# An attention and feed-forward kernel on one core: the planner's last slot of a round takes a VectorE step by its announced length

## The chip, the cores and the metric

One core of a Trainium2 chip runs the whole program. Times are device microseconds (us) of one execution. The kernel before took 1028.57 us, the median of 3 runs (1028.46 to 1028.59). The execution that the profiler recorded took 1029.18 us; its span, from the first to the last recorded instruction, is 1027.4 us, and the 1.78 us around it belong to no instruction of the program. A difference of under 0.2% (2.06 us) is called no change here.

## The reference

Two stages. The first is attention with a sigmoid in place of the softmax, for 8 batches, 12 heads, 448 positions and heads of 64 elements; the second is a feed-forward network over the 3584 rows that come out of it.

```
scores = scale * np.matmul(q, k.transpose(0, 1, 3, 2)) - np.log(S)
attn = 1.0 / (1.0 + np.exp(-scores))
attn_out = np.matmul(attn, v)                      # 8 x 12 x 448 x 64
x = attn_out.transpose(0, 2, 1, 3).reshape(B*S, H*D)   # 3584 x 768
h = x @ w_in                                       # 768 -> 2048
g = np.maximum(0.01 * h, h)
out = g @ w_out                                    # 2048 -> 768
```

All of it is float32. The kernel gets the weights as 64-bit words and decodes them itself.

## The kernel before

**Precision.** TensorE multiplies a rounded form of float32. Each operand is therefore split into a high part (a cast) and a low part (the operand less its high part), and a product is three matmuls: high by high, high by low, low by high. ScalarE makes most high parts, VectorE nearly all low parts (`low`, lines 202, 502, 607).

**Attention.** 48 pairs of heads are worked off in 24 rounds of two pairs (lines 794 to 814). Counted from 0, round r works on pairs 2r and 2r+1, called x and y, in five slots: scores of x, scores of y, x by its values, y by its values, and a last slot (`ending`) with the 64 positions that are left over of both. Scores go to PSUM in four buffers of two banks that are used in turn (tag `s`, line 767); a round takes nine of them: three for the scores of x, three for y, one each for the two products with the values, and one for the left-over scores. So the second score tile of a round takes the buffer in which the round before kept the product `pv` of its pair x. That buffer is free when VectorE has added it to the result in `keep` (lines 577 to 579), and the two `keep` additions of a round are put at the head of the next round's first slot (line 575). In slots 2 to 4 VectorE and ScalarE split the queries and keys of the next round's two pairs: the high part of the first in slot 2, its low part and the high part of the second in slot 3, the low part of the second in slot 4 (lines 805 to 807).

**The decoding.** Beside this VectorE decodes the weights, in the generator `prep` (lines 388 to 444). It is cut into steps, one VectorE instruction each, with a `yield` behind each. A weight block has four pieces; a piece takes three short instructions and two long ones on 128x384 words (lines 423 to 432). Behind the fourth piece of a `w_in` block come four long sums (`firsts`, lines 343 to 352), behind that of a `w_out` block a list of sums of 192, 384 or 576 words (`second`, lines 358 to 386). Some yields are free: they stand for no instruction, such as the nine behind each `w_in` block (`rest`). DMAs that load raw pieces and store results are issued by SyncE from inside the steps, and SyncE's queue keeps the program's order.

**The planner.** The program is written out in one order for each engine; nothing is reordered afterwards. Every VectorE instruction adds its length to a count called `queue`, by a formula: 0.14 us and its words at 960 or 1920 a us (lines 145 to 155). At the end of a slot `prepare(pace, time)` (lines 449 to 455) adds the pace to a credit, puts in steps while there is a credit of 1 and the count is more than 0.2 below the slot's time (`LESS`), and takes the slot's time off the count, down to zero at most. The slots' times are 1.92, 1.92, 2.33, 2.33 and 1.66. A step put in just under the limit may end well above it, and what is above the slot's time is carried into the next slot. After the attention, `fill` (lines 457 to 462) puts up to four steps into each of the products of the first matmul stage, by the same count against 1.8 us.

**After the attention.** The first matmul of the network is done in 4 quarters of 56 products of 9 matmuls with seven-product (Strassen) sums, the second in 52 products of 36 matmuls. Each weight tile of the first is cast and its low part taken about two products ahead.

Of the kernel before, what the change touches and what calls it, by code (L numbers as in the profile page):

```python
# [30 lines left out]
PACES = 4, 5, 4.2, 2.8, 2  # L31
TIMES = 1.92, 1.92, 2.33, 2.33, 1.66
PRODUCT, LESS, MOST = 1.8, 0.2, 4
WAIT, REST = 9, 3
FFN = 126
ALONE = 100
# [29 lines left out]
PLAIN = {0: (), 1: (("store", "d", 0, 4, 0),), 2: (("store", "d", 4, 2, 4),)}  # L66
STEPS = (
# [34 lines left out]
def attn_ffn_kernel(ctx: ExitStack, tc: tile.TileContext, qk, v, w_in, w_out, out):  # L102
# [40 lines left out]
    queue = 0.0  # L143
# [13 lines left out]
    def sub(to, x, y):  # L157
        vec(out=to, in0=x, in1=y, op=ALU.subtract)
# [10 lines left out]
    def later(slots, *fns, first=False):  # L169

        chores.setdefault(now + slots, ([], []))[not first].extend(fns)
# [162 lines left out]
    def block(dtype, shape, name, pool=None):  # L334

        pool, tag, size, bufs = pool or (pp, "w", 4 * HW, 2)
        a, b = shape
        t = pool.tile([P, size], F32, tag=tag, name=name, bufs=bufs)[:, :a * b]
        return (t if dtype == F32 else t.bitcast(dtype)).rearrange("p (a b) -> p a b", a=a, b=b)
# [3 lines left out]
    def firsts(u, dec):  # L343
        to = td[u // 2][:, :, u % 2]
        dma(out=to[:, :3], in_=dec[:, 1:])

        b12, b22, b11, b21 = (dec[:, i] for i in range(4))
        sums = block(F32, (4, HW), f"ws0_{u}")
        for place, x, y in ((2, b12, b11), (0, b22, sums[:, 2]), (1, b22, b12), (3, b21, sums[:, 0])):
            sub(sums[:, place], x, y)  # L350
            yield
        dma(out=to[:, 3:], in_=sums)

    def rest():

        return (None for _ in range(WAIT if now < FFN else REST))

    def second(u, k, dec):


        n = len(BLOCKS)
        size = wide // 2
        e, at = u // 2, u % 2 * size
        both = {side: dec[i].rearrange("p a b -> p (a b)").rearrange("p (n m) -> p n m", n=n) for i, side in enumerate("ds")}

        def of(n, side, at, step):
            x = both[side]
            if step == 0:
                return x[:, at:at + 1].broadcast_to((P, n, size))
            end = at + (n - 1) * step + (1 if step > 0 else -1)  # L370
            return x[:, at:end if end >= 0 else None:step]

        for what, *x in PLAIN.get(k, STEPS):
            if what == "wait":
                yield from rest()
            elif what == "store":
                side, i, n, form = x
                dma(out=t2d[:, form:form + n, e, at:at + size], in_=both[side][:, i:i + n])
            else:
                n, fn, *x = x  # L380
                to, x, y = (of(n, *z) for z in x)
                if fn == "neg":
                    vec_st(out=to, in0=x, scalar=-1.0, in1=y, op0=ALU.mult, op1=ALU.subtract)
                else:
                    (add if fn == "add" else sub)(to, x, y)
                yield

    def prep():

        n = 4
        pieces = [(m, k) for m in range(len(todo)) for k in range(n)]
        raws = []

        def load():
            at = len(raws)
            if at == len(pieces):
                return
            m, k = pieces[at]  # L400
            w, u = todo[m]
            size = 4 * HW // n
            pool = (stage, "stage", 2 * HW, STAGE) if at % 2 and now < ALONE else (pp, "wr", 2 * HW, 3)
            raw = block(I32, (size, 2), f"wr{w}_{u}_{k}", pool)
            dma(out=raw.rearrange("p m t -> p (m t)"), in_=(w_in, w_out)[w][u][:, k * size:(k + 1) * size].bitcast(I32))
            raws.append(raw)

        for _ in range(3):
            load()
        yield  # L410
        for at, (m, k) in enumerate(pieces):
            w, u = todo[m]
            if k == 0 and w == 0:
                dec = block(F32, (4, HW), f"wd{w}_{u}")
            elif k == 0:
                both = [block(F32, (4, HW), f"wd{w}_{i}") for i in range(2)] if u == 0 else both[::-1]
                dec = both[0]
            raw = raws[at]
            size = 4 * HW // n
            low, high = raw[:, :, 0], raw[:, :, 1]  # L420
            tf = dec.rearrange("p b m -> p (b m)")[:, k * size:(k + 1) * size]
            t = tf.bitcast(I32)
            vec_s(out=t, in0=high, scalar1=0x7FFFFFFF, scalar2=None, op0=ALU.bitwise_and)
            yield
            vec_s(out=tf, in0=tf, scalar1=W_LEAST, scalar2=W_MOST, op0=ALU.max, op1=ALU.min)
            yield
            vec_s(out=t, in0=t, scalar1=5, scalar2=2, op0=ALU.logical_shift_left, op1=ALU.logical_shift_right)
            yield
            vec_st(out=t, in0=high, scalar=-0x40000000, in1=t, op0=ALU.bitwise_and, op1=ALU.bitwise_or)
            yield  # L430
            vec_st(out=t, in0=low, scalar=29, in1=t, op0=ALU.logical_shift_right, op1=ALU.bitwise_or)
            yield
            while len(raws) < min(at + 1 + (5 if now < ALONE else 3), len(pieces)):
                load()
            if now < ALONE:
                yield
            if w == 1:
                yield from second(u, k, both)
            elif k == n - 1:
                yield from firsts(u, dec)  # L440
            if k == n - 1:
                prepared.add((w, u))
                if w == 0:
                    yield from rest()

    preps = prep()
    credit = 0.0

    def prepare(pace, time):
        nonlocal credit, queue  # L450
        credit += pace
        while credit >= 1 and queue < time - LESS:
            next(preps, None)
            credit -= 1
        queue = max(0.0, queue - time)

# [312 lines left out]
    def go(todo, work):  # L769


        for x, what in todo:
            for y in what.split():
                later(0, lambda x=x, y=y: x.do(y))
        slot(work)

    def whole(x):
        x.scores(0)
        x.scores(1)

    def ending(x, y):

        if y is not None:
            y.last_scores()
        x.last_v()
# [8 lines left out]
    for r in range(rounds):  # L794
        x, y, *more = pairs[2 * r:2 * r + 6]
        works = [lambda: whole(x), lambda: whole(y), x.attn_v, y.attn_v, lambda: ending(y, more[0] if more else None)]
        if r == 0:

            works = [works[2], works[1], x.last_scores, *works[3:]]
        if more:  # L800
            z, w = more[:2]
            how = vcopy if PLAN_ATTN.get((r, 3), "").startswith("h") else copy
            later(0, z.load_v)
            later(1, w.load_v)
            later(2, z.high)
            later(3, z.low, lambda: w.high(how))
            later(4, w.low)
        for n, far in enumerate(more[2:]):
            later(1 + 3 * n, far.load_qk)
        for n, work in enumerate(works):  # L810
            go([(ops[0], PLAN_ATTN.get((r, n), ""))], work)
            for t in EARLY.get((r - rounds + 1, n), ()):
                advance(t)
            prepare(PACES[n] * (r > 0), TIMES[n])

    kept, chores[now] = chores[now][0], ([], chores[now][1])
    for fn in kept:
# [20 lines left out]
    queue = 0.0  # L838
# [146 lines left out]
    ahead = 0  # L985
# [14 lines left out]
    ahead = READY + 2  # L1000

    for k in range(NOP, size):
        m, at = divmod(k - NOP, 12)
# [163 lines left out]
```

## Time and profile before

| what | us |
|---|---|
| median of 3 runs | 1028.57 |
| the profiled execution | 1029.18 |
| its span | 1027.4 |
| TensorE matmuls, busy | 1023.2 (100%) |
| TensorE weight loads, busy | 867.8 (84%) |
| VectorE, busy | 857.2 (83%) |
| ScalarE, busy | 598.1 (58%) |
| granted TensorE clock, mean | 1.000 |

TensorE's matmuls are pipelined and their ends are modelled, so that a gap of some tenths of a microsecond doesn't show in their busy time. The starts of the weight loads, one for each matmul, show it, and the profile says for each idle stretch of the weight loader what ended it; "issue" means that nothing it can see did. The attention fills the span up to 246 us, the first matmul of the network goes from there to 649 us, the second to 1024 us.

### The profile page before, as it was taken

How to read it: one execution, taken by the hardware profiler on the slowest of the kernel's cores; microseconds unless marked ns; L12 is line 12 of the kernel's file. 1: busy time of each engine (PE TensorE's matmuls, PEld its weight loads, DVE VectorE, ACT ScalarE, POOL GpSimd, SP SyncE). 2: the span in 40 equal slices, each digit the busy share in tenths (PEclk: the TensorE clock that was granted, in tenths of full speed). 3: DMA queues.
4: the chain of work that ended last, by engine and by line, in shares of the span. 5: the costliest groups of instructions: out<-in, count | busy, mean ns of one | idle time of the engine just before them, and what ended most of it. 6: DMA issues, size and time to landing. Idle time of an engine off the chain costs nothing.

```text
span 1027.4 us, 16361 instructions
## 1 busy us (share of the span) xinstructions
PE 1023.2 (100%) x6316; PEld 867.8 (84%) x6316; DVE 857.2 (83%) x1015; ACT 598.1 (58%) x634; POOL 0.3 (0%) x5
## 2 busy tenths in 40 slices
PE   9999999999999999999999999999999999999998
PEld 6555555556999999999999999999999999999998
DVE  5889999789998899898975657699988888899883
ACT  7888888887545655555555555565362535444440
POOL 0000000000000000000000000000000000000000
PEclk9999999999999999999999999999999999999999
DMA  8888787989889898989986878997678797767833
GB/s 308 279 298 278 280 281 267 311 292 331 289 312 322 293 298 299 344 317 409 338 296 213 300 283 313 392 408 289 217 282 286 278 416 291 284 221 252 311 113 135
DMA packets 113853, 301.10 MB, mean 293 GB/s; under 512 B 9712, under 2 KB 51696, under 8 KB 113776
## 3 DMA queue, kind: packets, MB, share of 16 engines
q1 hardware_dynamic: 111760, 295.52, 80.5%
q10 hardware_dynamic: 2016, 4.54, 1.2%
q8 instruction: 50, 0.82, 0.3%
q14 instruction: 27, 0.22, 0.1%
HBM read 203.16 MB, written 96.86 MB: 292 GB/s over the span
## 4 chain that ended last, share of the span: by engine, by line
PE 99%; ACT 0%; ACTq 0%; DVE 0%; DVEq 0%; issue 0%
PE px_h L139 22%; PE acc_A L139 18%; PE acc_B L139 18%; PE pv L139 13%; PE pz_h L139 11%; PE sc L139 11%; PE py_h L139 6%; PE acc_one L139 0%; ACTq L139 0%; ACT L139 0%; DVE o L139 0%; ACT qks L139 0%; DVEq L1163 0%; ACT warm L139 0%
## 5 line engine op out<-in xcount | busy, mean ns | idle before, releaser
L139 PE MATMUL px_h<-hi,w 128*128 128x448 f32 x768 | 223.1, 361 | 0.0
L139 PEld LDWEIGHTS px_h<-hi,w 128*128 128x128 f32 x768 | 143.9, 187 | 11.3 <-ACT x L139 0.7
L139 PE MATMUL acc_A<-gh,w 128*128 128x448 f32 x528 | 151.4, 361 | 0.0
L139 DVE TENSOR_TENSOR w<-wx,w 128x768 fp32r<-128x768 f32 x112 | 106.9, 955 | 48.2 <-ACT w L139 48.2
L139 PE MATMUL px_h<-lo,w 128*128 128x448 f32 x384 | 139.4, 363 | 0.0
L139 ACT ACTIVATE s<-sc 128x896 f32<-128x896 f32 x144 | 119.4, 934 | 17.7 <-PE sc L139 17.7
L139 PE MATMUL acc_B<-gh,w 128*128 128x448 f32 x416 | 119.4, 361 | 0.0
L139 PE MATMUL pv<-s,v 64*64 64x448 f32 x1152 | 114.0, 540 | 0.0
L139 PE MATMUL pz_h<-hi,w 128*128 128x448 f32 x384 | 112.7, 361 | 0.0
L139 PEld LDWEIGHTS acc_A<-gh,w 128*128 128x128 f32 x528 | 98.9, 187 | 7.4
L139 PEld LDWEIGHTS sc<-qks 64*128 64x128 f32 x876 | 79.9, 187 | 23.6 <-issue 16.2
L139 ACT CAST w<-wx 128x768 fp32r<-128x768 f32 x112 | 92.0, 834 | 10.8 <-DMA wx<-t 10.8
L139 PE MATMUL sc<-qks 64*128 64x448 f32 (+1 forms) x876 | 95.5, 368 | 0.1
L139 PEld LDWEIGHTS pv<-s,v 64*64 64x64 f32 x1152 | 41.6, 133 | 60.9 <-issue 47.7
L139 DVE TENSOR_TENSOR w<-w 128x1536 fp32r<-128x1536 f32 x52 | 91.1, 1752 | 0.0
L139 ACT ACTIVATE c_h<-c_h 128x896 f32<-128x896 f32 x48 | 45.9, 956 | 74.1 <-DVE c_h L139 74.1
L139 PE MATMUL acc_B<-g,w 128*128 128x448 f32 x328 | 84.8, 362 | 0.0
L139 PEld LDWEIGHTS acc_B<-gh,w 128*128 128x128 f32 x416 | 77.9, 187 | 5.8
L139 ACT CAST w<-w 128x1536 fp32r<-128x1536 f32 x52 | 77.1, 1482 | 0.5 <-DMA w<-t 0.5
L139 PEld LDWEIGHTS pz_h<-hi,w 128*128 128x128 f32 x384 | 71.9, 187 | 5.3
L139 PEld LDWEIGHTS px_h<-lo,w 128*128 128x128 f32 x384 | 72.1, 188 | 3.8
L139 DVE SCALAR_TENSOR_TENSOR wd<-wr,wd 128x384 int32<-128x384 int32 x128 | 71.3, 557 | 3.2
(96 smaller groups left out, 1619.1 us busy)
## 6 DMA issues: line engine op xcount, KB each, us to landing
wx<-t SPq DMA_DIRECT2D x112, 384.0 KB, 5.4
w<-t SPq DMA_DIRECT2D x52, 768.0 KB, 4.3
g<-g SPq DMA_DIRECT2D x34, 896.0 KB, 7.4
g<-c_h SPq DMA_DIRECT2D x60, 448.0 KB, 4.4
g<-s SPq DMA_DIRECT2D x48, 448.0 KB, 5.9
qk<-in_qk SPq DMA_DIRECT2D x46, 456.0 KB, 5.2
g1s<-g SPq DMA_DIRECT2D x18, 896.0 KB, 6.1
wr<-in_w_in SPq DMA_DIRECT2D x32, 384.0 KB, 5.2
```

What stands on the lines that cost most here:

```text
L139: return lambda *args, **kw: tc.keep_in_program_order(issue(*args, **kw))
```

## The change

Each step of the decoding announces how long the next one is: `LONG` (0.54) where the next is a long one, and nothing, which is read as `SHORT` (0.34), elsewhere. The announcement is kept in `ahead`. `prepare` gets a third argument, true in the last of a round's five slots. There a step is put in only if, beside the old condition, the count and the announced length together stay under the slot's time and 0.1 (`OVER`): under 1.76. Credit that is not spent stays. The other four slots and `fill` work as before, and the instructions are the same 1015 on VectorE, in another order.

```diff
+SHORT, LONG, OVER = 0.34, 0.54, 0.1
...
             sub(sums[:, place], x, y)
-            yield
+            yield LONG
...
-        for what, *x in PLAIN.get(k, STEPS):
+        steps = PLAIN.get(k, STEPS)
+        for m, (what, *x) in enumerate(steps):
...
-                yield
+                yield next((z[1] > 1 and LONG for z in steps[m + 1:] if z[0] == "sum"), None)
...
             vec_s(out=t, in0=t, scalar1=5, scalar2=2, op0=ALU.logical_shift_left, op1=ALU.logical_shift_right)
-            yield
+            yield LONG
             vec_st(out=t, in0=high, scalar=-0x40000000, in1=t, op0=ALU.bitwise_and, op1=ALU.bitwise_or)
-            yield
+            yield LONG
             vec_st(out=t, in0=low, scalar=29, in1=t, op0=ALU.logical_shift_right, op1=ALU.bitwise_or)
-            yield
+            yield k == n - 1 and LONG
...
             if now < ALONE:
-                yield
+                yield k == n - 1 and LONG
...
-    credit = 0.0
+    credit, ahead = 0.0, SHORT
 
-    def prepare(pace, time):
-        nonlocal credit, queue
+    def prepare(pace, time, whole):
+        nonlocal credit, queue, ahead
         credit += pace
-        while credit >= 1 and queue < time - LESS:
-            next(preps, None)
+        while credit >= 1 and queue < time - LESS and (not whole or queue + ahead < time + OVER):
+            ahead = next(preps, None) or SHORT
             credit -= 1
         queue = max(0.0, queue - time)
...
-            prepare(PACES[n] * (r > 0), TIMES[n])
+            prepare(PACES[n] * (r > 0), TIMES[n], n == len(works) - 1)
```

## Rows read from the trace of the kernel before

**Rows 1.** The page's first part: busy us (share) and instructions of each engine.

```profile
PE 1023.2 (100%) x6316; PEld 867.8 (84%) x6316; DVE 857.2 (83%) x1015; ACT 598.1 (58%) x634; POOL 0.3 (0%) x5
```

**Rows 2.** Busy time by stretch: window, PE, PEld, DVE, ACT, POOL (instructions), clock, DMA share, GB/s.

```profile
100.00:150.00 50.00, 50.00 (x502) 27.87 (x500) 46.60 (x83) 42.30 (x55) 0.00 (x0) 1.00 0.80 281
400.00:500.00 100.00, 100.00 (x502) 93.73 (x501) 91.47 (x129) 55.69 (x63) 0.00 (x0) 1.00 0.94 349
```

**Rows 3.** Waits of the weight loader, 0 to 260 us: total us, times, longest.

```profile
PEld sc L139 <- DVE x L139: 1.0, 4, 0.4
```

**Rows 4.** Weight loads in order of time: start, us, names, count, idle before and releaser.

```profile
106.40 3.51 PEld L139 LDWEIGHTS sc<-qks 64*128 64x128 f32 x36 [0.70 <-issue]
110.22 0.21 PEld L139 LDWEIGHTS pv<-s,v 64*64 64x64 f32 x8 [0.30 <-ACT s L139]
...
116.39 1.11 PEld L139 LDWEIGHTS sc<-qks 64*128 64x128 f32 x12 [0.70 <-issue]
117.74 2.32 PEld L139 LDWEIGHTS sc<-qks 64*128 64x128 f32 x24 [0.24 <-DVE x L139]
...
126.54 3.51 PEld L139 LDWEIGHTS sc<-qks 64*128 64x128 f32 x36 [0.70 <-issue]
...
136.52 1.11 PEld L139 LDWEIGHTS sc<-qks 64*128 64x128 f32 x12 [0.70 <-issue]
...
146.67 3.51 PEld L139 LDWEIGHTS sc<-qks 64*128 64x128 f32 x36 [0.71 <-issue]
...
176.63 1.11 PEld L139 LDWEIGHTS sc<-qks 64*128 64x128 f32 x12 [0.70 <-issue]
...
186.91 3.51 PEld L139 LDWEIGHTS sc<-qks 64*128 64x128 f32 x36 [0.71 <-issue]
...
236.86 1.11 PEld L139 LDWEIGHTS sc<-qks 64*128 64x128 f32 x12 [0.71 <-issue]
...
240.73 0.21 PEld L139 LDWEIGHTS pv<-s,v 64*64 64x64 f32 x8 [0.30 <-ACT s L139]
```

**Rows 5.** VectorE in order of time, round 9's end and the additions behind it.

```profile
105.59 1.03 DVE L139 TENSOR_TENSOR qks<-qk,qks 128x848 fp32r<-128x848 f32 x1
106.54 0.35 DVE L139 TENSOR_SCALAR wd<-wr 128x384 int32<-128x384 int32 x1
106.81 1.15 DVE L139 TENSOR_TENSOR x<-x,pv 128x448 f32<-128x448 f32 x2
```

**Rows 6.** VectorE, round 10's end and the additions behind it.

```profile
114.59 0.55 DVE L139 TENSOR_TENSOR ws<-wd 128x384 f32<-128x384 f32 x1
115.18 0.56 DVE L139 TENSOR_TENSOR ws<-wd,ws 128x384 f32<-128x384 f32 x1
115.65 1.03 DVE L139 TENSOR_TENSOR qks<-qk,qks 128x848 fp32r<-128x848 f32 x1
116.61 0.55 DVE L139 TENSOR_TENSOR ws<-wd 128x384 f32<-128x384 f32 x1
117.07 1.15 DVE L139 TENSOR_TENSOR x<-x,pv 128x448 f32<-128x448 f32 x2
```

**Rows 7.** VectorE early in the network's first matmul.

```profile
253.74 1.09 DVE L139 TENSOR_TENSOR c_h<-c_h,py_h 128x896 f32<-128x896 f32 x1 [0.82 <-PE py_h L139]
...
256.21 0.95 DVE L139 TENSOR_TENSOR w<-wx,w 128x768 fp32r<-128x768 f32 x1
```

**Rows 8.** The weight loads of product 6, from the first with the low part of its weights.

```profile
257.27 0.39 PEld L139 LDWEIGHTS pz_h<-hi,w 128*128 128x128 f32 x2
```

**Rows 9.** SyncE's queue in order of time, round 10.

```profile
114.70 0.38 SPq L139 DMA_DIRECT2D t<-wd  x1
115.17 0.44 SPq L139 DMA_DIRECT2D qk<-in_qk  x1
```

**Rows 10.** ScalarE, the cast that reads those queries and keys.

```profile
123.39 0.96 ACT L139 CAST qks<-qk 128x848 fp32r<-128x848 f32 x1
```

**Rows 11.** The page's DMA issues: count, KB each, median us from issue to landing.

```profile
qk<-in_qk SPq DMA_DIRECT2D x46, 456.0 KB, 5.2
```

## The prediction

> **What bounds the kernel now.** I read the page's shares first, then busy time by stretch, then what the weight loader waits for, and last its rows in order of time beside VectorE's. The shares name TensorE: 100% busy in matmuls, against 83% for VectorE [rows 1]. By stretch there are two kinds of time [rows 2]. In the network's matmuls 100 us hold 501 weight loads at 93.73 us of loader time; the stretches in between agree within one load, so nothing stalls there and no reordering can gain there. In the attention the loader is busy 27.87 of 50 us, since each of its load pairs is followed by a pause for the matmuls; here the starts must be read. The granted clock is 1.00, the 2.4 GHz level, in both.
>
> A round of attention is regular: from 106.40 to 116.39 us, 9.99 us, with a gap of 0.70 at its head that every round has [rows 4]. Of what the planner can change, one wait stands out: the loader waits for VectorE's `x` four times, 1.0 us in all, 0.4 at most [rows 3]. That is `keep`: the second score tile can't start until the old product is added and its buffer is free. The four rounds are 11, 13, 17 and 23. Round 11 stops after 12 loads for 0.24 us and lasts 126.54 - 116.39 = 10.15 us; round 13 lasts 146.67 - 136.52 = 10.15; round 17 lasts 186.91 - 176.63 = 10.28; round 23 needs 240.73 - 236.86 = 3.87 for its scores against 110.22 - 106.40 = 3.82 in round 10 [rows 4]. Over the regular length that is 0.16 + 0.16 + 0.29 + 0.05 = 0.66 us. This is the whole prize; even the listed wait, not netted against the slack behind it, is 1.0 us, or 0.1% of the run.
>
> **Why these four.** In round 11 the additions start at 117.07, 0.68 after the round's start, right behind a sum of the decoding at 116.61 [rows 6]. In round 10 they start at 106.81, 0.41 after, behind a short step at 106.54, and nothing waits [rows 4, 5]. So a start up to about 0.45 costs nothing, and each 0.1 us beyond costs 0.1. One long step moves them by 117.07 - 116.61 = 0.46.
>
> The planner's count says where this happens. A low part of 848 words counts 0.14 + 848/960 = 1.02, a short step 0.34, a long one 0.54. Round 10's last slot begins with 0.31 carried over and 1.02 of its own, together 1.34 before rounding; that is under 1.46, so the long sum goes in, to 1.88. Round 12 does the same; round 16 goes from 1.28 to 1.82, round 22 from 1.02 by a short step to 1.36 and by a long one to 1.90. Rounds 5, 8, 13 and 17 also end at 1.82 to 1.96 and nobody waits behind them, since their low part happened to start in time: the count sees the danger but not the exact lateness.
>
> **The change, part by part.** *The rule.* The limit becomes 1.76 for the end of a step. All eight of those steps would end above it and are refused. The short step of round 9 (1.25 to 1.59) would pass.
>
> *What the order becomes.* I carried both rules through all slots with the kernel's own formula. Up to round 5 the orders agree. From there the new one holds something back in 10 of the 23 last slots (rounds 5, 6, 8, 10 to 13, 15, 18, 22). Of the four that matter: round 10 holds its sum at 1.34, round 12 now begins at 1.25 and holds, round 22 holds its long step at 1.36. Round 16 begins at 1.25 with three decoding steps (c, d, e) between its low parts, and takes one short step to 1.59. That is the sequence at the end of round 9, and I give it that round's start, 0.41, so no wait [rows 5]. No last slot ends above 1.70, and the two at 1.70 have in front of them the same sequence as before. So the whole 0.66 goes, if each round behaves like its nearest row.
>
> *What comes back.* No instruction is removed. A held step opens the next round's first slot, behind `keep`, where nothing of TensorE waits for it. The credit saved (up to 14 against 9) fills the other slots no further than before, since the limit there is unchanged. The decoding falls behind by up to 2.1 us of count between rounds 10 and 18; then free steps take up the credit, and from slot 2 of round 19 to round 22's last slot the two orders are the same. VectorE must also fit its work into 9.99 us. By the distances between starts (0.95 for a low part, 1.06 for the pair of additions, 0.47 for a long step, 0.59 where the next needs its result, 0.27 to 0.39 for a short one [rows 5, 6]) I estimate 10.13 us for the old rounds 10 and 12, which is why they end late, and 9.98 at most for any new round (17). Tight, but not over.
>
> The Trainium skill has a rule against this, in "VectorE: DVE Perf Modes", section "The DRAIN you can't avoid": the next instruction does not start until the pipe of the one before has emptied. By it a step costs its full duration. Here it fails for independent neighbours, 0.47 us from start to start for an instruction of 0.56 (115.18 to 115.65), and holds for a dependent one, 0.59 (114.59 to 115.18) [rows 6]. What time it would give is the first rival.
>
> *SyncE.* Steps carry DMAs with them. The store of a decoded block and the loads behind it are issued in program order, so a store waiting for its step holds the loads of queries and keys. Round 10 shows it: the store leaves at 114.70, as its step ends, the load behind it at 115.17 [rows 9]; with the usual 5.2 us to land [rows 11] it is there at 120.4, and ScalarE reads it at 123.39 [rows 10], so 3.0 us are to spare. In the new order a last sum's store moves by at most one slot, about 2 us, and most of the moved ones now stand behind a load in the queue, not in front. Cost: nothing, up to 2 us of delay inside 3.0 of cover.
>
> *The start of the network.* The new order enters it one short step behind and is one ahead four slots later, so some 0.3 us more VectorE work stands in front of the addition at 253.74. That one waited 0.82 us for TensorE [rows 7], which covers it. Without that cover the low part that starts at 256.21 would end later than its 257.16; TensorE wants it at 257.27, 0.11 later [rows 7, 8]. So the cost is nothing, and at most 0.3 - 0.1 = 0.2 us. Further on the decoding runs up to 3 us of count ahead of the old order; the slots' limits are the same and the loader never stalls there. I take no change; below nothing there is no room either.
>
> **The sum.** Of the execution in the trace: 1029.18 - 0.66 = 1028.5, of which the span is 1026.7 and 1.78 lies around it. That execution lies 0.61 above the median of the runs, so against the median: 1028.57 - 0.66 = **1027.9 us**.
>
> **Rivals.** *The lateness moves.* If VectorE's steps cost their durations, the new round 17 has 7 short steps (2.5), 8 long ones (4.5), two additions (1.2) and two low parts (2.1), 10.3 us, 0.3 over a round, and rounds 9, 14, 16 and 20 come to some 10.2. Each would push `keep` past its 0.45 and about half of the prize would be paid in other rounds: 1028.2 to 1028.5. For it: the fill of the new rounds really is higher. Against it: round 20 is the same in both orders, comes to 10.2 as well by durations, and round 21 has no wait for VectorE; only four rounds have one [rows 3].
>
> *The change does nothing.* The waits stay because low parts start late from ScalarE's casts, not from the count: 1028.6. Against it, in round 10 the sum at 116.61 stands between the low part and the additions without a gap [rows 6].
>
> *Slower.* A store that waits for a postponed step holds SyncE, and a load of queries and keys behind it comes late. It decides once the extra delay is over 3.0 us, and makes the run slower than before from 3.7. A store that slips by a whole round, 9.99 us, in front of a load would cost 7.0 us: 1034.9. For it: it is one queue and the stores do move. Against it: they move by one slot.
>
> **How the numbers follow.** My case has a chance of 0.75 (own range 1027.6 to 1028.2), the moved lateness 0.13, no effect 0.07, the held queue 0.03; 0.02 is left for gains that no row shows. Low end: all of the 1.0 us of waits and 0.1 to 0.2 of scatter, 1027.4. High end: no effect and 0.1, 1028.7. A measurement can tell a change from about 0.2% on, 2.06 us; nearly all of this lies within: faster 0.02, same 0.95, slower 0.03.
>
> **What would show it.** In the changed kernel's weight loads rounds 11, 13, 17 and 23 should have 36 loads in one row and last 9.99 us; the wait for `x` should be gone or under 0.3 us in total. On VectorE the additions of round 11 should start near 116.6, straight behind the low part. Loads in the network's stretch should stay at 501 in 100 us. I am wrong if another round gains a wait for `x`, if a weight load waits for a cast of `qks`, or if the product at 257 stalls.

## The result, and the profile after

The changed kernel took 1038.56 us (median of 5 runs, 1036.75 to 1040.52) against 1028.59 for the kernel before (5 runs, 1028.46 to 1028.81): a ratio of 1.0094, with a 95% interval of [1.0082, 1.0105]; brackets behind other ratios mean the same. It is 10 us slower, where 1027.9 us, no change, was forecast. The execution in the trace took 1036.76 us, with a span of 1034.8; that is the low end of its runs, 7.4 above the span before.

The page's first part; the rows of before are [rows 1]:

```profile
PE 1024.4 (99%) x6316; PEld 868.6 (84%) x6316; DVE 857.4 (83%) x1015; ACT 597.6 (58%) x634; POOL 0.3 (0%) x5
```

The instructions are the same in number, and every engine is as busy as before to within 1.2 us. So the 7.4 us are nearly all waits, and the next view to read is what the weight loader waits for (total us, times, longest):

```profile
PEld acc_A L140 <- ACT o L140: 5.4, 1, 5.4
...
PEld sc L140 <- DVE x L140: 1.7, 2, 1.1
```

Before, the wait for `x` was four times, 1.0 in all [rows 3]; now it is two longer ones. The wait for `o`, a single one of 5.4 us, is new, and it is neither in the attention nor in the first matmul of the network. The weight loads in order of time, the first of each of rounds 11 to 14, 16 to 19, and then the place of the new wait (start, us, names, count, idle before and releaser; before: [rows 4]):

```profile
115.87 3.51 PEld L140 LDWEIGHTS sc<-qks 64*128 64x128 f32 x36 [0.71 <-issue]
...
125.85 3.51 PEld L140 LDWEIGHTS sc<-qks 64*128 64x128 f32 x36 [0.70 <-issue]
...
135.84 3.51 PEld L140 LDWEIGHTS sc<-qks 64*128 64x128 f32 x36 [0.70 <-issue]
...
145.83 3.51 PEld L140 LDWEIGHTS sc<-qks 64*128 64x128 f32 x36 [0.71 <-issue]
...
165.80 1.11 PEld L140 LDWEIGHTS sc<-qks 64*128 64x128 f32 x12 [0.70 <-issue]
167.60 2.31 PEld L140 LDWEIGHTS sc<-qks 64*128 64x128 f32 x24 [0.69 <-DVE x L140]
...
176.39 3.51 PEld L140 LDWEIGHTS sc<-qks 64*128 64x128 f32 x36 [0.70 <-issue]
...
186.38 1.11 PEld L140 LDWEIGHTS sc<-qks 64*128 64x128 f32 x12 [0.70 <-issue]
188.53 2.30 PEld L140 LDWEIGHTS sc<-qks 64*128 64x128 f32 x24 [1.05 <-DVE x L140]
...
197.31 3.51 PEld L140 LDWEIGHTS sc<-qks 64*128 64x128 f32 x36 [0.70 <-issue]
...
663.81 0.19 PEld L140 LDWEIGHTS acc_B<-gh,w 128*128 128x128 f32 x1
669.42 0.29 PEld L140 LDWEIGHTS acc_A<-gh,w 128*128 128x128 f32 x1 [5.42 <-ACT o L140]
...
671.08 0.70 PEld L140 LDWEIGHTS acc_A<-gh,w 128*128 128x128 f32 x2
...
672.20 0.70 PEld L140 LDWEIGHTS acc_A<-gh,w 128*128 128x128 f32 x2
```

Rounds 11 to 13 last 9.98 to 9.99 us: the stops of rounds 11 and 13 are gone, and so is the one of round 17 (176.39 to 186.38). Two rounds that were regular before now stop: round 16 (176.39 - 165.80 = 10.59) and round 18 (197.31 - 186.38 = 10.93; unrounded 10.94). With all rounds counted in this way, and with the stages behind them:

| stage | before | after | difference |
|---|---|---|---|
| to round 1's first load | 16.46 | 15.92 | -0.53 |
| rounds 11, 13, 17, 23 | | | -0.66 |
| rounds 16, 18 | | | +1.55 |
| first matmul of the network | 403.12 | 403.12 | 0.00 |
| second matmul | 374.20 | 381.27 | +7.07 |
| span | 1027.40 | 1034.84 | +7.44 |

(The first row's scatter over the runs told of below is 15.76 to 16.72, whatever the kernel.) So there are three effects: the forecast gain, a loss of 1.55 us in the attention, and a loss of 7.07 in one place of the second matmul, some 420 us after the last slot in which the rule holds a step back (round 22's, at 237 us). VectorE's order differs longer than that: the step held there shifts what comes behind it, and the two orders agree again only from 528 us on.

**The loss in the attention** stands in VectorE's rows. After, round 10's end, which answers to [rows 6] and is as forecast (the additions straight behind the low part, 0.21 after round 11's start), and then rounds 15 and 16:

```profile
115.13 1.03 DVE L140 TENSOR_TENSOR qks<-qk,qks 128x848 fp32r<-128x848 f32 x1
116.08 1.15 DVE L140 TENSOR_TENSOR x<-x,pv 128x448 f32<-128x448 f32 x2
...
158.07 1.15 DVE L140 SCALAR_TENSOR_TENSOR wd<-wr,wd 128x384 int32<-128x384 int32 x2
159.14 0.55 DVE L140 TENSOR_TENSOR ws<-wd 128x384 f32<-128x384 f32 x1
...
160.67 0.55 DVE L140 TENSOR_TENSOR ws<-wd,ws 128x384 f32<-128x384 f32 x1
162.97 0.37 DVE L140 TENSOR_SCALAR wd<-wr 128x384 int32<-128x384 int32 x1 [1.75 <-DMA t<-wd]
...
166.93 1.15 DVE L140 TENSOR_TENSOR x<-x,pv 128x448 f32<-128x448 f32 x2
```

and SyncE's store of that block:

```profile
159.25 0.38 SPq L140 DMA_DIRECT2D t<-wd  x1
```

Before, the same steps:

```profile
156.60 0.55 DVE L139 SCALAR_TENSOR_TENSOR wd<-wr,wd 128x384 int32<-128x384 int32 x1
157.07 1.15 DVE L139 TENSOR_TENSOR x<-x,pv 128x448 f32<-128x448 f32 x2
158.13 0.55 DVE L139 TENSOR_TENSOR ws<-wd 128x384 f32<-128x384 f32 x1
...
160.67 0.37 DVE L139 TENSOR_SCALAR wd<-wr 128x384 int32<-128x384 int32 x1 [0.46 <-DMA t<-wd]
```

The decoded blocks and their four sums take turns in two buffers (`bufs=2`, tag "w"), so the next block's first step writes the buffer whose store has just been issued behind the last decoding step, and must wait until it has landed. Before, the two `keep` additions stood between that last step and the sums, 158.13 - 157.07 = 1.06 us of useful work, and the wait was 0.46. After, the held steps all come behind `keep`, in one stretch, the sums follow the step at once, and the wait is 1.75. VectorE has lost 1.3 us and starts round 16's additions 166.93 - 165.80 = 1.13 after the round's start, where up to about 0.45 costs nothing. A second block leads to the stop of round 18: its next first step starts 3.6 us after its store is issued (183.30 - 179.69), against 3.7 here (162.97 - 159.25). The profile names no releaser for that wait of 1.64, so that the store is the cause there too is shown only by the experiments below.

**The loss in the second matmul** stands in ScalarE's rows. After:

```profile
651.33 3.58 ACTq L140 DMA_DIRECT2D g<-s  x4
654.95 1.69 ACT L140 CAST gh<-g1s 128x1792 fp32r<-128x1792 f32 x1 [4.02 <-DMA g<-c_h]
...
665.72 3.64 ACT L140 COPY o<-acc_A 128x1344 f32<-128x1344 f32 x3 [7.49 <-DMA g<-s]
```

and before:

```profile
657.46 3.63 ACT L139 COPY o<-acc_A 128x1344 f32<-128x1344 f32 x3
```

How long the four stores took from issue to landing, after:

```profile
DMA to landing us min/median/max: 4.3/8.3/11.9
```

and before:

```profile
DMA to landing us min/median/max: 4.5/8.4/11.9
```

The copy empties the first accumulator of the second matmul into its first output tile `o`. After, it waits for one of four stores of intermediates of the first matmul (`g<-s`, 448 KB each), which ScalarE has just issued; TensorE needs the accumulator again at 664, and stands still until 669.4. A copy waits for a store of something else only if it writes where the store still reads. The compiled programs give the addresses. The framework hands the seven buffers of the pool `st` (one for each of 116 intermediate tiles of the first matmul) to the tiles when the program is built. In the two programs 65 of the 116 have another buffer, from one exchanged pair of neighbours on; every other tile lies where it lay. The first output tile lies over two of these seven buffers. In the old program their last users were two tiles `c_h`, whose stores left at 648.2 and 650.6 and landed 5.2 and 3.8 us later, the second at 654.4, 3 us before the copy starts. In the new one they are two sums, `s0` and `s7`, and `s7` is the last of the four stores in ScalarE's queue. That store leaves at 653.7 and lands at 665.6. In the old program it was as late (its slowest store, too, took 11.9 us), but the first output tile did not lie over it.

By stretch (window, PE, PEld, DVE, ACT, POOL, clock, DMA share, GB/s):

```profile
664.00:668.00 4.00, 0.37 (x2) 0.00 (x0) 0.63 (x1) 2.28 (x2) 0.00 (x0) 0.80 1.03 428
668.00:672.00 4.00, 2.58 (x7) 2.32 (x8) 1.02 (x1) 4.00 (x4) 0.00 (x0) 0.50 1.01 422
672.00:676.00 4.00, 4.00 (x19) 3.69 (x18) 4.00 (x3) 2.87 (x3) 0.00 (x0) 0.85 1.01 421
```

When TensorE goes on the granted clock is 0.50, the 1.2 GHz level, and ten matmuls start 0.373 us apart (three loads from 671.08 to 672.20) in place of 0.200 [rows 2]: 10 x 0.173 = 1.7 us more. The stop and the ten slow matmuls, 5.4 + 1.7, are the 7.07. The length of the stop hangs on when a store lands among others (the DMA share is 1.0 there): here the last took 11.9 us and TensorE stood for 5.4, in a trace shown below (`late`) 15.4 and 8.6. The runs of this kernel lie 3.8 us apart, where those of before lie 0.4.

### The profile page after: what moved, and what is told of

The parts are those of the page before. It is cut to its first block, busy times and chain, and to the rows that moved or that the text cites. A ratio compares the mean times of both kernels' runs of the same rounds, so it can differ in the third digit from the quotient of the medians.

```text
span 1034.8 us, 16359 instructions
## 1 busy us (share of the span) xinstructions
PE 1024.4 (99%) x6316; PEld 868.6 (84%) x6316; DVE 857.4 (83%) x1015; ACT 597.6 (58%) x634; POOL 0.3 (0%) x5
## 4 chain that ended last, share of the span: by engine, by line
PE 91%; DMA 4%; DVE 2%; ACT 1%; issue 1%; SPq 0%; DVEq 0%; ACTq 0%
PE px_h L140 20%; PE acc_A L140 18%; PE acc_B L140 17%; PE pv L140 11%; PE pz_h L140 10%; PE sc L140 10%; PE py_h L140 5%; DMA wx<-t 1%; DMA g<-s 1%; DMA g<-c_h 1%; DMA v<-in_v 0%; PE acc_one L140 0%; DVE wd L140 0%; DVE qks L140 0%; DMA t<-wd 0%
## 5 line engine op out<-in xcount | busy, mean ns | idle before, releaser
L140 PE MATMUL acc_A<-gh,w 128*128 128x448 f32 x528 | 154.0, 366 | 5.0 <-ACT o L140 5.0
```

The lines of the kernel that those rows point to most:

```text
L140: return lambda *args, **kw: tc.keep_in_program_order(issue(*args, **kw))
```

## The experiments

The theory: two mechanisms that have nothing to do with each other. S (store): the closed-up steps meet the store of their block, +1.55 us. H (hand-out): another choice of buffers puts the first output tile under a tile that is stored late, +7 and more. The rivals: one of the two is a consequence of the other; the stop in the second matmul comes from the decoding's being ahead or behind, not from the buffers; and, for the attention, the rival of the prediction by which lateness comes from VectorE's steps costing their durations.

### Half of the rule: rounds before 22, and from 22 on

`early`:

```diff
-            prepare(PACES[n] * (r > 0), TIMES[n], n == len(works) - 1)
+            prepare(PACES[n] * (r > 0), TIMES[n], n == len(works) - 1 and r < 22)
```

> The new rule in rounds 0 to 21 only; round 22's last slot goes by the old one, so the network's stage begins with the same VectorE order as before. Theory (buffers): the 7.1 us at the start of the second matmul come from the places of the intermediate tiles, which only the step held in round 22 turns over; here they are as before, and what is left is the attention's own balance, 0.6 gained in rounds 11, 13, 17 against 0.6 and 0.95 lost in rounds 16 and 18: 1029.0 to 1029.6 us, no wait for ScalarE's o. Rival (order): the moved decoding steps and their DMAs crowd the seam; nearly all moved steps are here, so 1036 to 1040.

`late`:

```diff
+            prepare(PACES[n] * (r > 0), TIMES[n], n == len(works) - 1 and r >= 22)
```

> The new rule in rounds 22 and 23 only: one long step held, everything up to there as before. Theory (buffers): this alone turns the tiles' places over, and the first output copy waits for the last store of the first matmul: a stall of some 5.4 us and some us at half clock, 1035.5 to 1040 us, and attention rounds 16 and 18 stay at 9.99. Rival (order): one long step of 0.56 us can't crowd anything: 1028.5.

Measured: early 1030.12 (1029.23 to 1030.72, 10 runs), ratio 1.0011 [1.0002, 1.002]; late 1036.96 (1036.93 to 1040.64, 4 runs), 1.0087 [1.007, 1.0103]; the kernel before beside them 1028.96.

The two halves are not of the size that was expected. VectorE's 1015 instructions stand in another order than before in 436 places; early has 101 of these, from 66 to 198 us, and late 335, from 237 to 528 us, since the one step that round 22 holds shifts what comes behind it. So late differs from the kernel before in more than one step, and these two runs alone can't tell the order from the hand-out; the runs with a written list below can.

Early has the stops of the attention and none in the second matmul (374.20), and ScalarE's copy begins without a wait:

```profile
166.39 1.11 PEld L140 LDWEIGHTS sc<-qks 64*128 64x128 f32 x12 [0.70 <-issue]
168.20 2.32 PEld L140 LDWEIGHTS sc<-qks 64*128 64x128 f32 x24 [0.69 <-DVE x L140]
```

```profile
659.05 3.62 ACT L140 COPY o<-acc_A 128x1344 f32<-128x1344 f32 x3
```

Late has rounds 11, 13 and 17 as in the kernel before (10.15, 10.13, 10.27) and the stop in the second matmul, 8.6 us in the execution that was traced (1040.64, its highest), and one more in the first matmul:

```profile
PEld acc_A L140 <- ACT o L140: 8.6, 1, 8.6
...
PEld px_h L140 <- DVE w L140: 1.3, 1, 1.3
```

The second begins on VectorE, again at a buffer of the pool `st` from which a store is still under way:

```profile
283.68 1.09 DVE L140 TENSOR_TENSOR s<-s,c_h 128x896 f32<-128x896 f32 x1 [2.92 <-DMA g<-c_h]
```

The changed kernel, with the same order and hand-out there, has no such wait in its trace; why this execution had it is not shown.

So S and H come apart, and for H it is enough that round 22's last slot holds its step. In the compiled programs early has the hand-out of before, late that of the changed kernel. Early missed what was expected of it by 0.5: the upper end was 1029.6. Against the 1028.96 beside it the difference is 1.16, and its trace accounts for that: +1.61 in rounds 16 and 18, -0.61 in rounds 11, 13 and 17, and +0.14 in round 23, which still waits there (9.43, against 9.29 before).

### The hand-out alone

The pool `st` becomes seven pools of one buffer, and a written list says which of them each tile gets: list A is the old program's choice, list B the new one's. Nothing else moves; both kernels' orders can be built with either list.

```diff
+SLOTS = "01234562350162301425301264502163021650421560431564021354012634026351426354203154236014326543261403214065214603521605"
...
-            t = self.pool.tile([P, 2, S], F32, tag=self.tag, name=f"{what}_{self.name}", bufs=self.bufs)
+            t = self.pool[next(slots)].tile([P, 2, S], F32, tag=self.tag, name=f"{what}_{self.name}", bufs=1)
...
-                new = st.tile([P, 2, S], F32, tag="st", name=f"{x}_{p}_{u}", bufs=ST)
+                new = st[next(slots)].tile([P, 2, S], F32, tag="st", name=f"{x}_{p}_{u}", bufs=1)
...
-    st = left.enter_context(tc.tile_pool(name="st", bufs=ST, reuse_waits="tile"))
+    st = {x: left.enter_context(tc.tile_pool(name=f"st{x}", bufs=1, reuse_waits="tile")) for x in "0654321"}
+    slots = iter(SLOTS)
```

That is list A. List B:

```diff
+SLOTS = "01234562305162351402351064250163501625401265431264503124530614506123406124015324056134506245063415034162034615203612"
```

The old order with list B (`before_pinB`):

> The kernel before, every instruction in its old order; only the seven buffers of the intermediate tiles are handed out by a written list, the one that the changed kernel got. Theory (buffers): as slow at the start of the second matmul as the changed kernel, 1035.5 to 1040 us. Rival (order): no step is moved, so 1028.6.

The new order with list A (`after_pinA`):

> The changed kernel with the seven buffers handed out by the list that the kernel before got. Theory (buffers): no stall at the second matmul, 1029.0 to 1029.6 us, with the waits in rounds 16 and 18 still there. Rival (order): 1036 to 1040.

The control, the old order with list A (`before_pinA`):

> Control: the kernel before, its seven buffers handed out by a written list that repeats what it got anyway. Every theory: the time of the kernel before, within 0.3 us. If it differs, the written list has a price of its own and the two runs with lists must be read against this one.

Measured:

| order, list | us | ratio to before | second matmul |
|---|---|---|---|
| old, B | 1037.09 (1036.47 to 1037.63, 4 runs) | 1.0077 [1.006, 1.0094] | 382.64 |
| new, A | 1029.89 (1029.36 to 1032.8, 10 runs) | 1.0015 [1.0006, 1.0025] | 374.20 |
| old, A | 1028.67 (1028.31 to 1029.12, 11 runs) | 0.9998 [0.9989, 1.0007] | 374.20 |

The weight loader's waits of the old order with list B, an order in which no instruction is moved:

```profile
PEld acc_A L141 <- ACT o L141: 6.3, 1, 6.3
PEld sc L141 <- DVE x L141: 0.8, 3, 0.4
```

and of the new order with list A:

```profile
PEld sc L142 <- DVE x L142: 1.7, 2, 1.0
```

```profile
657.93 3.63 ACT L142 COPY o<-acc_A 128x1344 f32<-128x1344 f32 x3
```

The hand-out alone makes the old order 8 us slower, and taking it back makes the new one 8.7 us faster. The control shows that seven pools of one buffer cost nothing. What the new order has left is S: 1029.89 - 1028.96 = 0.9 us, the +1.55 less the 0.66. Its time lies 0.3 above the range expected of it, but the kernel before, too, was 0.4 slower in these runs than when it was first measured. Four of its ten runs lie at 1031.0 to 1032.8, which no trace explains. That the decoding is ahead or behind is excluded as a cause of the stop.

### Which part of the hand-out

Lists A and B differ in 65 places. If it is the overlap of two addresses, exchanging two buffers' names throughout, without a change in who follows whom, must move the stop. `after_relabel` is the new order with list B and the digits 2 and 0 exchanged, so that `s7` lies elsewhere; `before_under` is the old order with list A and the digits 5 and 2 exchanged, so that `s7` comes under the first output tile. For after_relabel:

```diff
-SLOTS = "01234562305162351402351064250163501625401265431264503124530614506123406124015324056134506245063415034162034615203612"
+SLOTS = "21034560325160351420351264052163521605421065431064523104532614526103426104215304256134526045263415234160234615023610"
```

and for before_under:

```diff
-SLOTS = "01234562350162301425301264502163021650421560431564021354012634026351426354203154236014326543261403214065214603521605"
+SLOTS = "01534265320165301452301564205163051620451260431264051324015634056321456324503124536014356243561403514062514603251602"
```

> The changed kernel with its own hand-out of the seven buffers, tile for tile, but with the addresses of two buffers exchanged, so that the tile that is stored last lies away from the first output tile. Theory (overlap): what costs 7 us and more is only that these two share an address; no stall at the second matmul, 1029.4 to 1030.2 us as with the old list. Rival (rotation): the changed hand-out itself delays stores within the first matmul; 1036 to 1040 as before the exchange.

> The kernel before with its own hand-out, tile for tile, and the addresses of two buffers exchanged, so that the tile that is stored last lies under the first output tile. Theory (overlap): a stall of 5 to 9 us at the second matmul and some us at half clock, 1035.5 to 1040. Rival (rotation): 1028.9.

Measured: after_relabel 1029.82 (1029.48 to 1030.21, 10 runs), 1.0007 [0.9998, 1.0017]; before_under 1038.83 (1038.2 to 1039.31, 4 runs), 1.0095 [1.0081, 1.0108]; the kernel before beside them 1028.98. ScalarE's copy in after_relabel:

```profile
660.68 3.65 ACT L142 COPY o<-acc_A 128x1344 f32<-128x1344 f32 x3 [3.29 <-DMA g<-s]
```

and in before_under, with the weight loader's wait that follows from it:

```profile
668.28 3.64 ACT L141 COPY o<-acc_A 128x1344 f32<-128x1344 f32 x3 [10.85 <-DMA g<-s]
```

```profile
PEld acc_A L141 <- ACT o L141: 8.2, 1, 8.2
```

It is the overlap. In after_relabel the copy still waits for one of the stores, but an earlier one; with 3.29 us it is done before TensorE needs the accumulator, and the second matmul takes 374.21. In before_under nothing but two names of buffers differs from the control, and it is 10 us slower. The compiled programs agree: in after_relabel the first output tile lies over `s0`, the first of the four stores, in before_under over `s7`.

### The store and the two buffers

If S is right, a third buffer for the sums removes both stops of the attention, and does nothing for the old order. `after_three` is the new order, list A, with a buffer of their own for the sums; `before_three` the old order with the same:

```diff
+    own = attn.enter_context(tc.tile_pool(name="own", bufs=1))
...
-        sums = block(F32, (4, HW), f"ws0_{u}")
+        sums = block(F32, (4, HW), f"ws0_{u}", (own, "own", 4 * HW, 1))
```

> The changed kernel with the old places of the intermediate tiles, and the four sums of a decoded block in a buffer of their own, so that the next block's first step needs no buffer whose store is under way; the order of the instructions is that of the changed kernel. Theory (store): rounds 16 and 18 lost 0.6 and 0.95 us because that first step, now only four sums behind the store, waited 1.6 to 1.75 us for it to land; here they last 9.99, rounds 11, 13 and 17 too, and the time is 0.5 to 0.7 us under the kernel before. Rival (durations, the first rival of the prediction): the new rounds are too full, so rounds 16 and 18 stay long and the time stays at 1029.9, 0.9 above.

> The kernel before with the sums' own buffer and no new rule. If the rule is what empties rounds 11, 13 and 17, they stay at 10.15 to 10.28 us here and the time stays that of the kernel before, within 0.3 us. If the buffer alone does it (the two waits of 0.46 us that the kernel before has for a store lead up to late additions), some of them shorten, up to 0.3 us.

`after_cap` is the new order, list A, with two buffers as before, and a bound on the credit that may be saved, so that the held steps come back in smaller groups:

```diff
-        credit += pace
+        credit = min(credit + pace, 12)
```

> The changed kernel with the old places of the intermediate tiles and its credit held to 12 at most, so that the nine free steps behind a block don't all go at once and the next block's first step comes later. Theory (store): by the distances between starts the first step then comes 5 us behind the store in the two blocks in question, not 2.1, so no wait: 0.4 to 0.7 us under the kernel before. Rival (durations): no help, 1029.5 or more.

Measured, beside 1028.92 for the kernel before (33 runs):

| kernel | us | ratio to before | rounds over 10.1 us |
|---|---|---|---|
| after_three | 1028.33 (1027.76 to 1028.78, 11 runs) | 0.9994 [0.9985, 1.0003] | none |
| before_three | 1028.96 (1028.27 to 1029.62, 11 runs) | 1.0001 [0.9992, 1.0009] | 11, 13, 17 |
| after_cap | 1028.51 (1028.08 to 1029.18, 11 runs) | 0.9997 [0.9988, 1.0006] | none |

VectorE in after_three, at the place of the 1.75 us:

```profile
161.44 0.55 DVE L142 TENSOR_TENSOR ws<-wd,ws 128x384 f32<-128x384 f32 x1
161.91 0.35 DVE L142 TENSOR_SCALAR wd<-wr 128x384 int32<-128x384 int32 x1
...
166.78 1.15 DVE L142 TENSOR_TENSOR x<-x,pv 128x448 f32<-128x448 f32 x2 [0.45 <-PE pv L142]
```

and its rounds 16 to 18:

```profile
166.58 3.51 PEld L142 LDWEIGHTS sc<-qks 64*128 64x128 f32 x36 [0.70 <-issue]
...
176.57 3.51 PEld L142 LDWEIGHTS sc<-qks 64*128 64x128 f32 x36 [0.70 <-issue]
...
186.56 3.51 PEld L142 LDWEIGHTS sc<-qks 64*128 64x128 f32 x36 [0.71 <-issue]
...
196.54 3.51 PEld L142 LDWEIGHTS sc<-qks 64*128 64x128 f32 x36 [0.70 <-issue]
```

The next block's first step follows the last sum without a wait, and `keep` starts 0.20 after round 16's start, so early that it waits for TensorE. Every round from 4 on is 9.98 to 9.99 long (round 3 has 10.06 in both kernels). The 0.66 us of the prediction are then there without a loss: against the kernel before, after_three has -0.59 where the new order with list A alone had +0.93, 1.5 us for the two stops. In before_three rounds 11, 13 and 17 keep their stops; the gain is the rule's and not the buffer's. after_cap shows that the two buffers do no harm where the steps come back in another grouping; but it pays 0.4 us at one product of the network's first matmul:

```profile
PEld pz_h L142 <- DVE w L142: 0.4, 1, 0.4
```

That is the low part for product 6, with 0.11 us to spare before [rows 7, 8].

### The best version, again

after_three was run once more, with another chip's runs of the kernel before beside it (`after_three_again`, no edit):

> The version with the sums' own buffer and the old list once more, to narrow its difference from the kernel before, which came out as 0.6 us less with an interval that reached over zero. Theory (store): 0.4 to 0.8 us under the kernel before. Rival: the gain of 0.67 us in the rounds is eaten by scatter at the program's start, 0 to 0.3.

Measured: 1028.36 (1027.79 to 1029.55, 11 runs) beside 1028.98 (21 runs), 0.9994 [0.9985, 1.0002]. Twice 0.6 us below the kernel before, as the 0.66 would have it, but each interval reaches over 1: by the bound of this document it is no change. No version seen here beats the kernel before measurably.

## Why the prediction was wrong

**The step that failed** is "The start of the network", at "Further on the decoding runs up to 3 us of count ahead of the old order; the slots' limits are the same and the loader never stalls there. I take no change". It treats the program as the same tiles at the same addresses with some VectorE instructions elsewhere. The order in which instructions are written out also decides which buffer a tile gets, and the order that came of one held step changed 65 of 116. The second matmul got no term of its own and so stood at 0; it measured +7.07 us in the trace, and some 7 to 11 over the runs, if all of their scatter lies here. No row that the prediction reads shows the danger: that the loader never stalled in the old program said that this hand-out was harmless, not that any would be. Why the framework's choice turns on this one step was not tried; that it depends on the order is shown by the compiled programs of `early` and `late`.

**The second step that failed** is "What comes back", at "A held step opens the next round's first slot, behind `keep`, where nothing of TensorE waits for it". No engine waits for the steps themselves, but they are a chain with a DMA in it: a step that closes up to its predecessor comes nearer to the landing of the predecessor's store. The term was 0 and measured +1.55 (rounds 16 and 18); the prediction's own sign of being wrong, that another round gains a wait for `x`, came true there. The estimate of 9.98 us of VectorE work at most in a new round had no wait in it; without the wait, in after_three, no round from 4 on lasts longer than 9.99.

**What was right.** The four waits of rounds 11, 13, 17 and 23 and their price of 0.66 us: all four are gone in the changed kernel, and after_three shows the sum by itself (-0.59 and -0.62, within what the runs scatter). SyncE's queue cost nothing, and neither did the start of the network: the first matmul lasts 403.12 in both kernels. In the kernel before, the danger of [rows 6] was read correctly as one long step.

**The rivals.** "The lateness moves" is told from S by after_three: it has the same order, the same 15 steps in round 17, and every round is regular; the additions of round 16 that were 1.13 late are 0.20 late when only the wait for the store is taken away. The start-to-start distance of independent steps is 0.47 us there too (161.44 to 161.91) for an instruction of 0.55, so these neighbours don't cost their durations. The prediction cites against itself a rule of the Trainium skill ("VectorE: DVE Perf Modes", section "The DRAIN you can't avoid"), that the next instruction does not start until the pipe has emptied. The same section says that a next operation that is not held starts earlier. With that the trace agrees. "The change does nothing" falls with the four waits. "Slower" came true, but not by its mechanism: it had SyncE held by a store that waits for a step, and no weight load waits longer for a cast of `qks` than before; what happened is a step, and a copy, that wait for a store.

The chance of 0.03 for slower was too small. It priced one known queue and left nothing for what the edit does to the allocation.

## What to carry to other kernels

In a program whose buffers are handed out by the order of the code, an edit that moves one instruction is two edits, and the second can be the larger: compare the addresses of all tiles before and after, look for tiles of the next stage that lie over buffers stored last, and pin the hand-out to measure an order by itself. A step that writes a rotating buffer has a distance to keep from the store that empties it; work that stands between the two by chance is cover, and a rule that closes steps up takes it away.

## What the runs showed of the hardware

Four stores of 448 KB, issued from one queue within 2.4 us at a DMA share of 1.0, landed 4.3 to 11.9 us after their issue (median 8.3), so the last to land held its buffer for almost three times as long as the quickest. And a stop of TensorE cost 1.6 to 2.1 us more than its length: in the four traces with one (the changed kernel, before_pinB, before_under and late) TensorE stood for 5.4, 6.3, 8.2 and 8.6 us, the granted clock was at 0.50 when it went on, and the next 10, 12, 9 and 10 matmuls started 0.373 us apart in place of 0.200.
